# A fused attention and two-layer network: units of 256 tokens, then pairs of 512 with part of g in the place of w_in

## The chip, the cores and the metric

One core of one Trainium2 chip. The metric is device time in microseconds (us) of one execution, from the start of the program to its end; a kernel's time is the median of several runs. The core has TensorE (PE: matmuls; its weight loads are shown as PEld), VectorE (DVE), ScalarE (ACT), GpSimd (POOL) and SyncE (SP), which issues the DMAs here.

## What is computed

Attention with positive random features, then a network of two layers on every token. Cut to what matters:

```python
# q, k, v: [8 batches, 8 heads, 576 tokens, 64]; omega: [128, 64]
def phi(x):                       # x scaled by 64 ** -0.25
    h = x @ omega.T - sum(x * x) / 2
    return exp(h - max(h)) / sqrt(128)
kv = einsum('bhsm,bhsd->bhmd', phi(k), v); z = sum over s of phi(k)
attn = einsum('bhsm,bhmd->bhsd', phi(q), kv) / (phi(q) . z + 1e-6)
x = attn as [4608 tokens, 512]
h = x @ w_in                      # w_in: [512, 2048]
out = (h - tanh(h)) @ w_out       # w_out: [2048, 512]
```

## The kernel before

The 4608 tokens are 18 units of 256 (`TC`), four chunks of 128 features (`NC`) each. w_in and w_out together are 16 tiles `wt[f]` of 128 partitions, each with a coarse part (index 0) and a fine part (index 1) of two float32r numbers whose sum is the weight; a part's first 512 words are a block of w_in (128 columns of h), its last 512 a block of w_out. They are loaded packed (`raw`) and decoded on ACT, DVE and POOL (`decode`, L439 to L451) in the first 160 us.

**The attention** of the later units is made of steps that run beside the network. A `k_unit` (one batch, one chunk; `k_single` after the first two batches) makes the sums kv and z; a `q_unit` (one unit, one chunk) makes 128 features of x for 256 tokens, and `x_split` writes them as a coarse and a fine part into `xh` and `xl` (L406, L407), which hold two units. A k step and a q step are generators: each `yield` ends a stage, and `beat()` lets every running step make one stage. The table `start` says at which beat a step begins; a unit of the network takes 16 beats, and units 0 and 1 are done as one.

**The network** of a unit: `ffn_h` (L468) makes two tiles of h, f = 2s and 2s+1, in 24 matmuls of 256 columns (4 chunks x 3 products x 2 tiles; the weights are `wt`, x is what streams). tanh (ACT, L472), h - tanh(h) (DVE, L473), the coarse part gh (ACT, L474) and the fine part gl (DVE, L475) follow. `ffn_out` (L486 to L488) multiplies g of the step before with w_out: 12 matmuls of 512 columns, into the two output tiles `po0` and `po1` of 128 tokens. Each of the 8 banks of PSUM has its tag. Units 0 and 1, in which no attention needs PSUM any more, are one unit of 512 tokens: one tile of h is 12 matmuls of 512 columns, and there are four output tiles.

**The order of the work** is made by a scheduler, which keeps the program's meaning and sets the order on each engine; each engine then runs in that order, and so does the queue of DMAs on SP.

In a unit, x must be whole before its first tile of h:

```python
while ch > 2 and xdone.get(ch, 0) < NC:
    tick((), True)
g = (ch, s, *ffn_h(ch, s))
```

Of the kernel before, what the change touches and what calls it, by code (L numbers as in the profile page):

```python
# [19 lines left out]
P = 128  # L20
# [1 line left out]
NF = DFF // P  # L22
NS = NF // 2
TC = 256
NCH = NT // TC
E = D + 2
SCALE = float(D) ** -0.25
EPS = 1e-6 * M
# [3 lines left out]
def favor_attention_ffn(ctx: ExitStack, tc: tile.TileContext, qT, kT, va, vt, omT, w, out):  # L32
# [283 lines left out]
    def q_unit(ch, c):  # L316
# [47 lines left out]
        if native:  # L364
            qf = att("qt", [P, 2, TC], F32, f"qt_{n}")
            nc.scalar.copy(qf.rearrange("p h t -> p (h t)"), pt)
            yield
            pn = ps.tile([P, TC], F32, tag=bank("pt"), name=f"pn_{n}")
            for b, s, e in pieces:
                for h in range(2):  # L370
                    nc.tensor.matmul(pn[:, s:e], kvf[b][c][:, h], qf[:, h, s:e], start=h == 0, stop=h == 1)
            if ch == 2:
                if c < 2:
                    x2[c] = sb.tile([P, TC], F32, tag="xs", name=f"x2_{c}", bufs=2)
                elif c == 2:
                    x2[3] = sb.tile([P, DM], F32, tag="o", name="x2")
                    x2[2], x2[3] = x2[3][:, 0:TC], x2[3][:, TC:]
                nc.scalar.copy(x2[c], pn)
# [112 lines left out]

    def ffn_store(ch):
        for t, p in enumerate(pos[ch]):
            if ch == NCH - 1 and t == 1:
                o = sb.tile([P, DM], F32, tag="g", name=f"o_{ch}_{t}")
                nc.vector.tensor_copy(o, p)
            else:
                o = sb.tile([P, DM], F32, tag="o", name=f"o_{ch}_{t}")
                nc.scalar.copy(o, p)
            r = ch * TC + t * P  # L500
            nc.sync.dma_start(out[r : r + P, :], o)
# [50 lines left out]
    while decoded < NF:  # L552
# [26 lines left out]
    mode.update(  # L579
        chain=False, native=False, norm=[nc.vector, nc.vector, nc.vector, nc.scalar], junk=[junk],  # L580
        hi=nc.scalar, pj=["pj0"], pk=["pk"], pt=["pj0"],
        phi=(ak, 3), qh=(ak, 1), ql=(ak, 1), tmp=(ak, 1), kf=(ak, 1), kx=(ak, 1), qf=(ak, 2),
        qx=(ak, 1), vr=(ak, 1), khl=(ak, 2), vhl=(ak, 2), zs=(ak, 1), c1=(ak, 1), kvs=(ak, 1))
# [6 lines left out]
    for b in range(2, B):  # L592
        for c in range(NC):
# [3 lines left out]
    assert min(start) >= t  # L597
# [6 lines left out]
    for s in range(done, NF):  # L604
        step(s, beat)
    for c in range(NC):
        x_split(2, c, x2[c], nc.vector)
    ffn_out(*prev)
    ffn_store(0)
    mode.update(pj=["pj0", "pj1"], pt=["pt"])  # L610
    prev = None
    for ch in range(2, NCH):
        out_tiles(ch)
        for s in range(NS):
            while ch > 2 and xdone.get(ch, 0) < NC:
                tick((), True)
            g = (ch, s, *ffn_h(ch, s))
            beat()
            if prev is not None:
                ffn_out(*prev)  # L620
                if s == 0:
                    ffn_store(ch - 1)
            beat()
            prev = g
    ffn_out(*prev)
    ffn_store(NCH - 1)
    for name in list(pools)[::-1]:
        close_pool(name)

# [34 lines left out]
```

## Time and profile before

| | before |
|---|---|
| median of 3 runs | 1071.04 us (1069.25 to 1071.6) |
| the profiled execution, its own time | 1070.01 us |
| its span in the profile | 1068.2 us |
| PE busy | 1044.0 us (98%), 6760 matmuls |
| PEld busy | 949.3 us (89%) |
| DVE busy | 854.0 us (80%) |
| ACT busy | 713.2 us (67%) |
| POOL busy | 323.5 us (30%) |
| DMA | 55.91 MB, mean 52 GB/s |

Times in the profile are counted from the start of the span. PE's matmuls overlap (the end of one is modelled), so the time that one takes in a row of them is read from start to start, not from its duration. DVE's short operations overlap too: its busy time is less than the sum of their durations. The granted clock (PEclk) is a share of full speed: 1.00 is 2.4 GHz, 0.50 is 1.2 GHz. A group of instructions has the line, engine, operation, out<-in, shape and count, then busy us, mean ns of one, and the idle time before them with what ended it.

### The profile page before, as it was taken

How to read it: one execution, taken by the hardware profiler on the slowest of the kernel's cores; microseconds unless marked ns; L12 is line 12 of the kernel's file. 1: busy time of each engine (PE TensorE's matmuls, PEld its weight loads, DVE VectorE, ACT ScalarE, POOL GpSimd, SP SyncE). 2: the span in 40 equal slices, each digit the busy share in tenths (PEclk: the TensorE clock that was granted, in tenths of full speed). 3: DMA queues.
4: the chain of work that ended last, by engine and by line, in shares of the span. 5: the costliest groups of instructions: out<-in, count | busy, mean ns of one | idle time of the engine just before them, and what ended most of it. 6: DMA issues, size and time to landing. Idle time of an engine off the chain costs nothing. (4 is left out here: it accounts for less than half of the span.)

```text
span 1068.2 us, 20318 instructions
## 1 busy us (share of the span) xinstructions
PE 1044.0 (98%) x6760; PEld 949.3 (89%) x6760; DVE 854.0 (80%) x3030; ACT 713.2 (67%) x1833; POOL 323.5 (30%) x553
## 2 busy tenths in 40 slices
PE   8988999989999999999999999999999999999998
PEld 7767888988999999999999998999999999999997
DVE  6999985898888986788888888898888897666522
ACT  6997655777676765577777766777767775555422
POOL 4634540344333320133333333233333331000000
PEclk8999999998999999999999999999999999999999
DMA  8750401111111110011111111111101110000000
GB/s 266 234 212 12 178 4 48 43 43 38 33 53 33 53 33 31 11 53 33 52 34 52 34 28 53 33 48 29 51 22 52 29 41 11 30 11 26 1 21 20
DMA packets 35529, 55.91 MB, mean 52 GB/s; under 512 B 12256, under 2 KB 21600, under 8 KB 33376
## 3 DMA queue, kind: packets, MB, share of 16 engines
q1 hardware_dynamic: 35344, 54.57, 16.2%
q8 instruction: 54, 0.88, 0.4%
q14 instruction: 51, 0.42, 0.1%
q10 hardware_dynamic: 80, 0.03, 0.0%
HBM read 45.15 MB, written 9.44 MB: 51 GB/s over the span
## 5 line engine op out<-in xcount | busy, mean ns | idle before, releaser
L468 PE MATMUL h<-xh,w 128*128 128x256 f32 (+1 forms) x2176 | 453.3, 292 | 3.8 <-DVE g L473 2.1
L468 PEld LDWEIGHTS h<-xh,w 128*128 128x128 f32 x2176 | 356.7, 191 | 14.1 <-DVE g L473 2.7
L468 PE MATMUL h<-xl,w 128*128 128x256 f32 (+1 forms) x1088 | 317.3, 292 | 0.5 <-DVE xl L407 0.5
L486 PE MATMUL po<-w,gh 128*128 128x512 f32 x544 | 214.2, 394 | 0.0
L468 PEld LDWEIGHTS h<-xl,w 128*128 128x128 f32 x1088 | 207.9, 191 | 6.7 <-DVE xl L407 0.8
L487 PE MATMUL po<-w,gh 128*128 128x512 f32 x544 | 213.7, 393 | 0.0
L488 PE MATMUL po<-w,gl 128*128 128x512 f32 x544 | 209.3, 391 | 0.0
L473 DVE TENSOR_TENSOR g<-h,g 128x512 f32<-128x512 f32 x144 | 98.8, 686 | 66.4 <-ACT g L472 65.3
L472 ACT ACTIVATE g<-h 128x512 f32<-128x512 f32 x144 | 85.1, 591 | 99.2 <-PE h L468 91.9
L474 ACT CAST gh<-g 128x512 fp32r<-128x512 f32 x144 | 89.4, 621 | 84.3 <-DVE g L473 82.7
L475 DVE TENSOR_TENSOR gl<-g,gh 128x512 fp32r<-128x512 f32 x144 | 109.9, 764 | 38.3 <-ACT gh L474 36.5
L488 PEld LDWEIGHTS po<-w,gl 128*128 128x128 f32 x544 | 102.2, 188 | 20.7
L486 PEld LDWEIGHTS po<-w,gh 128*128 128x128 f32 x544 | 102.5, 188 | 16.6
L487 PEld LDWEIGHTS po<-w,gh 128*128 128x128 f32 x544 | 102.5, 188 | 15.2
L347 DVE CUSTOM_DVE_ANT_0 junk<-phi_q,zb 128x128 f32<-128x128 f32 (+1 forms) x320 | 96.5, 303 | 14.7 <-ACT phi_q L150 0.5
L250 POOL TENSOR_TENSOR khl<-phi_ka,khl 128x256 fp32r<-128x256 f32 x48 | 38.0, 795 | 154.2 <-DVE khl L249 129.2
L150 ACT ACTIVATE phi_q<-phi_q,nb_q 128x128 f32<-128x128 f32 x240 | 79.0, 392 | 6.3 <-DVE nb_q L146 6.1
L258 POOL CAST vhl<-v 128x128 fp32r<-128x128 f32 (+1 forms) x144 | 45.7, 319 | 100.9 <-PE pk L266 82.4
L439 POOL TENSOR_SCALAR a<-a 128x1024 f32<-128x1024 f32 x14 | 59.0, 4214 | 54.7 <-ACT a L435 42.1
L387 DVE TENSOR_TENSOR ql<-pt,qh 128x512 fp32r<-128x512 f32 x60 | 41.1, 685 | 26.5 <-ACT qh L386 26.1
L259 DVE TENSOR_TENSOR vhl<-v,vhl 128x128 fp32r<-128x128 f32 (+1 forms) x144 | 45.2, 314 | 16.7 <-POOL vhl L258 13.0
L146 DVE CUSTOM_DVE_ANT_0 phi_q<-pj_q,phi_q 128x128 f32<-128x128 f32 x240 | 55.9, 283 | 1.1 <-ACT phi_q L143 1.0
(151 smaller groups left out, 1952.9 us busy)
## 6 DMA issues: line engine op xcount, KB each, us to landing
raw<-w SPq DMA_DIRECT2D x16, 1024.0 KB, 7.5
kf<-kT SPq DMA_DIRECT2D x32, 288.0 KB, 2.9
qf<-qT SPq DMA_DIRECT2D x72, 128.0 KB, 2.1
out<-o SPq DMA_DIRECT2D x36, 256.0 KB, 2.0
v<-vt SPq DMA_DIRECT2D x24, 288.0 KB, 2.8
v<-va SPq DMA_DIRECT2D x8, 288.0 KB, 5.8
omf<-omT ACTq DMA_DIRECT2D x1, 32.0 KB, 2.1
omf<-omT SPq DMA_DIRECT2D x1, 32.0 KB, 2.4
```

The lines of the kernel that those rows point to most:

```text
L146: nc.vector.tensor_tensor_reduce(ph[:, j], pj[:, i, :M], ph[:, j], scale=-SCALE, scalar=3.0e38, op0=ALU.add, op1=ALU.min, accum_out=nb[:, ...
L150: nc.scalar.activation(ph[:, j], ph[:, j], AF.Exp, bias=nb[:, j : j + 1], scale=-1.0)
L347: nc.vector.tensor_tensor_reduce(bank("junk")[r], ph[r, i], kvs[b, c][1][r, h], scale=1.0, scalar=EPS, op0=ALU.mult, op1=ALU.add, accum_ou ...
L439: engine.tensor_scalar(a.bitcast(F32), a.bitcast(F32), 2.0**-15, 122879.9921875, op0=ALU.max, op1=ALU.min)
L468: nc.tensor.matmul(o, w_, x, start=i == 0, stop=i == len(prods) - 1)
L472: nc.scalar.activation(g, p, AF.Tanh)
L473: nc.vector.tensor_sub(g, p, g)
L474: nc.scalar.copy(gh, g)
L475: nc.vector.tensor_sub(gl, g, gh.bitcast(F32))
L486: nc.tensor.matmul(po[t], h, wt[f][:, 0, DM:], start=first, stop=False)
L487: nc.tensor.matmul(po[t], h, wt[f][:, 1, DM:], start=False, stop=False)
L488: nc.tensor.matmul(po[t], l, wt[f][:, 0, DM:], start=False, stop=last)
```

## The change

Units 0 to 5 (`C0` = 6) stay as they are. The other twelve become six pairs of 512 tokens (`NL`). In a pair, `wide_h` makes one tile of h for all 512 tokens, in 12 matmuls of 512 columns. PSUM has room for two output tiles only, so `wide_out` adds up the output of the pair's first 256 tokens while h is made (6 matmuls of 512 columns per tile of h), and g of the other 256 tokens is kept until h is done: POOL writes its coarse and fine parts over the first half of the block of w_in that has just been used (`wt[f][:, i, 0:TC]`). Two runs of 48 matmuls, one for each of the other two output tiles, follow (`products`). So that the next pair finds w_in again, `w_in_away` stores w_in in DRAM during unit 2, and `w_in_back` loads each block, about six tiles ahead, into the second halves of w_in's places, which hold eight blocks (`NB`).

x of a pair is collected in a new tile `later`; `next_x` splits it when all eight q steps of the pair are there, after the h of the pair before. The table `start` is another one; a pair has 40 beats. Some buffers go or shrink to make room: `xs`, `tmp`, `o` (output tiles of units 0 to 5 use the buffers of gl and gh), `qf` from 2 to 1, `kvw` from 7 to 6.

```diff
-                    xs = sb.tile([P, TC], F32, tag="xs", name=f"xs_{n}", bufs=2)
+        while ch >= C0 and gathered < (ch - C0) // 2:
+            yield
+        xs = later[:, c, ch % 2 * TC : ch % 2 * TC + TC]
...
+    def w_in_away(f):
+        w_dram[f] = tc.dram_tile([P, 2, DM], F32, name=f"w_in{f}")
+        nc.sync.dma_start(w_dram[f], wt[f][:, :, 0:DM].bitcast(F32))
+    def w_in_back(i):
+        f, k = i % NF, 2 * (i % NB)
+        for j in range(2):
+            for a in range(2):
+                nc.sync.dma_start(wt[k + j][:, a, TC:DM].bitcast(F32), w_dram[f][:, a, TC * j : TC * j + TC])
...
+    def wide_h(a, f):
+        p = ps.tile([P, 2, TC], F32, tag=bank("h"), name=f"h_w{a}_{f}")
+        prods = [(w_in(a, f, i, c), x[:, 0:2, c]) for c in range(NC)
+                 for i, x in ((0, xh), (0, xl), (1, xh))]
+        for i, (w_, x) in enumerate(prods):
+            nc.tensor.matmul(p, w_, x, start=i == 0, stop=i == len(prods) - 1)
...
+        nc.scalar.activation(g, p, AF.Tanh)
+        nc.vector.tensor_sub(g, p, g)
+        nc.scalar.copy(e[:, 0], g[:, 0])
+        nc.vector.tensor_sub(e[:, 1], g[:, 0], e[:, 0].bitcast(F32))
+        hi, lo = [wt[f][:, i, 0:TC] for i in range(2)]
+        nc.gpsimd.tensor_copy(hi, g[:, 1])
+        nc.gpsimd.tensor_sub(lo, g[:, 1], hi.bitcast(F32))
...
-            k = 28 + 4 * c if ch == 3 else 42 + 4 * c if ch == 4 else 16 * (ch - 1) - 6 + 4 * c
+            if ch < C0 + 2:
+                k = [(28,32,36,40),(41,45,49,53),(56,60,63,66),(58,68,72,75),(78,81,83,85)][ch - 3][c]
+            else:
+                k = begins(a - 1) + -9 + 10 * (j + c) // 2
             start.setdefault(k, []).append(("q", ch, c))
...
-            k = 31 + 5 * c if b == 2 else 16 * (need[b] - 1) - 25 + 8 * c
+            k = [31,51][b - 2] + [5,5][b - 2] * c if b < 2 + len([31,51]) else begins(a - 1) + -18 + 11 * c
...
+    next_x(0)
+    for a in range(NL):
+        r = (C0 + 2 * a) * TC
+        out_tiles("w")
+        prev = None
+        for f in range(NF):
+            g = wide_h(a, f)
+            beat()
+            if prev is not None:
+                wide_out(*prev)
+            i = NF * a + f + 6
+            if NF <= i < NF * NL:
+                w_in_back(i)
+            beat()
+            prev = g
+        wide_out(*prev)
+        for i in range(2):
+            store(pos["w"][i], r + i * P)
+        for i in range(2):
+            p = ps.tile([P, DM], F32, tag=bank("h"), name=f"last_{a}_{i}")
+            for f in range(NF):
+                products(p, f, *[wt[f][:, j, i * P : (i + 1) * P] for j in range(2)])
+                if f % 4 == 3:
+                    beat()
+            store(p, r + (2 + i) * P, nc.vector if a == NL - 1 and i == 1 else nc.scalar)
+            if i == 0 and a < NL - 1:
+                next_x(a + 1)
```

How the scheduler sets the changed program shows in two places. On PE, at the start of unit 6 before (`po` are output tiles of unit 5, `h` is unit 6's first tile):

```order
L486 MATMUL po_5_4427<-w_1525,gh_6_5045 128x512
L487 MATMUL po_5_4427<-w_1525,gh_6_5045 128x512
L488 MATMUL po_5_4427<-w_1525,gl_6_5046 128x512
L468 MATMUL h_0_5170<-xh,w_219 128x256
L468 MATMUL h_0_5170<-xl,w_219 128x256
L468 MATMUL h_0_5170<-xh,w_219 128x256 x2
L363 MATMUL pt_0_5154<-ident,phi_q_0_5066 128x128
L468 MATMUL h_0_5170<-xl,w_219 128x256
L363 MATMUL pt_0_5154<-ident,phi_q_0_5066 128x128 x3
```

and on PE at the start of the first pair now (`h_w_0` and `h_w_1` are the pair's first two tiles of h, `po` again those of unit 5, `pt` a transpose of a later q step; `w_1569` is the tile f = 14):

```order
L532 MATMUL h_w_0_5642<-xl,w_220 128x512
L532 MATMUL h_w_0_5642<-xh,w_220 128x512
L532 MATMUL h_w_1_5705<-xh,w_337 128x512
L532 MATMUL h_w_1_5705<-xl,w_337 128x512
L532 MATMUL h_w_1_5705<-xh,w_337 128x512
L489 MATMUL po_5_4743<-w_1569,gh_7_5538 128x512
L490 MATMUL po_5_4743<-w_1569,gh_7_5538 128x512
L489 MATMUL po_5_4744<-w_1569,gh_7_5538 128x512
L490 MATMUL po_5_4744<-w_1569,gh_7_5538 128x512
L366 MATMUL pt_2_5267<-ident,phi_q_2_5086 128x128 x4
L532 MATMUL h_w_0_5642<-xh,w_220 128x512
L532 MATMUL h_w_1_5705<-xh,w_337 128x512
```

Before, unit 6's first tile of h followed in the order of its chunks, with nothing but the transposes of one q step among it; now the first pair's first two tiles stand in pieces of a chunk or less, and matmuls of unit 5's last step and of attention have been moved between them.

On SP, the loads of the packed weights f = 8 to 11 before (`qf` is a load for a q step):

```order
L81 DMA raw_987<-w 128x1024
L81 DMA qf_3_1041<-qT 128x256
L81 DMA raw_1084<-w 128x1024
L81 DMA raw_1139<-w 128x1024
L81 DMA raw_1249<-w 128x1024
```

and the same place now (`w_in` is w_in's copy in DRAM, stored from the decoded tiles f = 4 to 7):

```order
L84 DMA raw_1082<-w 128x1024
L512 DMA w_in_2042<-w_743 256x1x512
L512 DMA w_in_2044<-w_905 256x1x512
L512 DMA w_in_2203<-w_983 256x1x512
L512 DMA w_in_2205<-w_1078 256x1x512
L84 DMA raw_1137<-w 128x1024
```

Four stores, each of which needs a decoded tile, stand ahead of the load of f = 10 now.

## Rows read from the trace of the kernel before

**Rows 1.** Page, part 1: busy us (share of the span) and instructions of two engines.

```profile
PE 1044.0 (98%) x6760; PEld 949.3 (89%) x6760; DVE 854.0 (80%) x3030; ACT 713.2 (67%) x1833; POOL 323.5 (30%) x553
```

**Rows 2.** Timeline of PE at 1000 us: start, length, line, operation, count.

```profile
1000.03 0.28 PE L468 MATMUL h<-xl,w 128*128 128x256 f32 x1
...
1001.47 0.28 PE L468 MATMUL h<-xl,w 128*128 128x256 f32 x1
```

**Rows 3.** Timeline of PE in units 0 and 1 (512 tokens), one tile of h.

```profile
128.11 0.39 PE L468 MATMUL h<-xh,w 128*128 128x512 f32 x1
...
130.83 0.39 PE L486 MATMUL po<-w,gh 128*128 128x512 f32 x1
```

**Rows 4.** Timeline of PE at unit 3's start; in brackets the idle time before.

```profile
239.54 0.50 PE L142 MATMUL pj_kb<-om,kx 128*128 128x256 f32 x2 [2.82 <-DVE nb_km L146]
...
241.69 1.09 PE L363 MATMUL pt<-ident,phi_q 128*128 128x128 f32 x4 [1.15 <-DVE xs L400]
```

**Rows 5.** Timeline of DVE: the last chunks of x of units 3 and 6.

```profile
245.78 0.43 DVE L407 TENSOR_TENSOR xl<-xs,xh 128x256 fp32r<-128x256 f32 x1
...
409.18 0.42 DVE L407 TENSOR_TENSOR xl<-xs,xh 128x256 fp32r<-128x256 f32 x1
```

**Rows 6.** Timeline of PE: unit 6's first matmul.

```profile
411.77 0.28 PE L468 MATMUL h<-xh,w 128*128 128x256 f32 x1
```

**Rows 7.** Windows: us, busy of PE, PEld, DVE, ACT, POOL, clock, DMA share, GB/s.

```profile
50.00:100.00 50.00, 41.66 (x223) 33.27 (x222) 49.41 (x162) 42.07 (x114) 18.07 (x8) 1.00 0.32 119
202.60:245.80 43.20, 38.59 (x250) 34.67 (x248) 39.63 (x157) 32.66 (x92) 19.71 (x40) 0.94 0.16 48
245.80:409.20 163.40, 162.94 (x1112) 151.62 (x1113) 142.74 (x559) 114.37 (x308) 56.55 (x109) 0.98 0.14 39
500.00:900.00 400.00, 399.46 (x2742) 370.44 (x2741) 347.47 (x1370) 286.84 (x774) 143.33 (x278) 1.00 0.13 38
900.00:1000.00 100.00, 100.00 (x666) 91.98 (x666) 64.31 (x241) 55.53 (x138) 0.00 (x0) 1.00 0.06 18
245.00:250.00 5.00, 4.47 (x21) 4.18 (x21) 4.92 (x15) 2.71 (x9) 3.52 (x6) 0.50 0.47 121
```

**Rows 8.** Windows of line L400 alone (DVE): one operation for each q step.

```profile
245.80:409.20 163.40, 5.13 (x12) 0.98 0.14 39
900.00:1000.00 100.00, 2.99 (x7) 1.00 0.06 18
```

**Rows 9.** Windows of line L313 alone (DVE): one operation for each k step.

```profile
245.80:409.20 163.40, 2.08 (x6) 0.98 0.14 39
```

**Rows 10.** Windows of line L475 alone (DVE): one for each two tiles of h.

```profile
245.80:409.20 163.40, 17.58 (x23) 0.98 0.14 39
900.00:1000.00 100.00, 11.08 (x16) 1.00 0.06 18
```

**Rows 11.** Page, part 5: the work on h, in groups of the whole run.

```profile
L473 DVE TENSOR_TENSOR g<-h,g 128x512 f32<-128x512 f32 x144 | 98.8, 686 | 66.4 <-ACT g L472 65.3
L472 ACT ACTIVATE g<-h 128x512 f32<-128x512 f32 x144 | 85.1, 591 | 99.2 <-PE h L468 91.9
L474 ACT CAST gh<-g 128x512 fp32r<-128x512 f32 x144 | 89.4, 621 | 84.3 <-DVE g L473 82.7
L475 DVE TENSOR_TENSOR gl<-g,gh 128x512 fp32r<-128x512 f32 x144 | 109.9, 764 | 38.3 <-ACT gh L474 36.5
```

**Rows 12.** Page, part 5: two groups of POOL.

```profile
L250 POOL TENSOR_TENSOR khl<-phi_ka,khl 128x256 fp32r<-128x256 f32 x48 | 38.0, 795 | 154.2 <-DVE khl L249 129.2
...
L258 POOL CAST vhl<-v 128x128 fp32r<-128x128 f32 (+1 forms) x144 | 45.7, 319 | 100.9 <-PE pk L266 82.4
```

**Rows 13.** Timeline of DVE: the last operation of decoding f = 7.

```profile
99.19 1.22 DVE L451 SCALAR_TENSOR_TENSOR w<-m,a 128x1024 fp32r<-128x1024 uint32 x1
```

**Rows 14.** Timeline of ACT: the first operation of decoding f = 10.

```profile
108.18 1.15 ACT L435 ACTIVATE a<-raw 128x1024 f32<-128x1024 f32 x1
```

**Rows 15.** Page, part 6: loads of packed weights, KB each, us to landing.

```profile
raw<-w SPq DMA_DIRECT2D x16, 1024.0 KB, 7.5
```

More of the change, by code (lines that the diff above doesn't have):

```diff
@@ L24 @@
 TC = 256
-NCH = NT // TC
+NQ = NT // TC
+C0 = 6
+NL = (NQ - C0) // 2
+NB = 8
 E = D + 2
@@ L372, in q_unit @@
             if ch == 2:
[L373 to L378, printed above, removed]
+                nc.scalar.copy(later[:, c, 0:TC], pn)
             else:
@@ L456, in favor_attention_ffn @@
     xh, xl = [sb.tile([P, 2, NC, TC], F32R, name=f"x{k}") for k in "hl"]
+    later = sb.tile([P, NC, 2 * TC], F32, name="later")
     def ffn_h(ch, s):
@@ L493, in ffn_store, with store @@
         for t, p in enumerate(pos[ch]):
[L494 to L501, printed above, removed]
+            store(p, ch * TC + t * P)
+    def store(p, r, engine=nc.scalar):
+        o = sb.tile([P, DM], F32, tag=bank("o"), name=f"o_{r}", bufs=1 if mode["o"][-1] == "g" else 2)
+        copy(engine, o, p)
+        nc.sync.dma_start(out[r : r + P, :], o)
@@ L503, in out_tiles, with products, wide_out @@
+    def products(o, f, h, l):
+        nc.tensor.matmul(o, h, wt[f][:, 0, DM:], start=f == 0, stop=False)
+        nc.tensor.matmul(o, h, wt[f][:, 1, DM:], start=False, stop=False)
+        nc.tensor.matmul(o, l, wt[f][:, 0, DM:], start=False, stop=f == NF - 1)
+    def wide_out(a, f, h, l):
+        for t, p in enumerate(pos["w"]):
+            products(p, f, h[:, t * P : (t + 1) * P], l[:, t * P : (t + 1) * P])
     def out_tiles(ch, tags=("po0", "po1")):
@@ L508, in favor_attention_ffn @@
     xdone = {}
-    x2 = {}
+    gathered = 0
     gens = []
@@ L581, in favor_attention_ffn, with begins @@
         hi=nc.scalar, pj=["pj0"], pk=["pk"], pt=["pj0"],
[L582 removed]
+        phi=(ak, 3), qh=(ak, 1), ql=(ak, 1), kf=(ak, 1), kx=(ak, 1), qf=(ak, 1),
         qx=(ak, 1), vr=(ak, 1), khl=(ak, 2), vhl=(ak, 2), zs=(ak, 1), c1=(ak, 1), kvs=(ak, 1))
     start = {}
[L588 removed]
+    def begins(a):
+        return 16 * C0 + 40 * a
+    for ch in range(3, NQ):
+        a, j = (ch - C0) // 2, (ch - C0) % 2 * NC
         for c in range(NC):
[L590 removed]
+            if ch < C0 + 2:
+                k = [(28,32,36,40),(41,45,49,53),(56,60,63,66),(58,68,72,75),(78,81,83,85)][ch - 3][c]
+            else:
+                k = begins(a - 1) + -9 + 10 * (j + c) // 2
             start.setdefault(k, []).append(("q", ch, c))
     for b in range(2, B):
+        a = ((b * S) // TC - C0) // 2
         for c in range(NC):
[L594 removed]
+            k = [31,51][b - 2] + [5,5][b - 2] * c if b < 2 + len([31,51]) else begins(a - 1) + -18 + 11 * c
             start.setdefault(k, []).append(("k", b, c))
     t = 32 - 2 * (NF - done)
[L597 removed]
+    assert min(start) >= t and all(k == int(k) for k in start)
     def beat():
@@ L606, in favor_attention_ffn @@
     for c in range(NC):
-        x_split(2, c, x2[c], nc.vector)
+        x_split(2, c, later[:, c, 0:TC], nc.vector)
     ffn_out(*prev)
@@ L611, in favor_attention_ffn @@
     prev = None
-    for ch in range(2, NCH):
+    for ch in range(2, C0):
         out_tiles(ch)
@@ L622, in favor_attention_ffn @@
                     ffn_store(ch - 1)
+            if ch == 2:
+                for f in range(2 * s, 2 * s + 2):
+                    w_in_away(f)
             beat()
@@ L625, in favor_attention_ffn, with next_x @@
     ffn_out(*prev)
-    ffn_store(NCH - 1)
+    ffn_store(C0 - 1)
+    mode.update(o=["g", "gl"])
+    def next_x(a):
+        nonlocal gathered
+        for ch in (C0 + 2 * a, C0 + 2 * a + 1):
+            while xdone.get(ch, 0) < NC:
+                tick((), True)
+        gathered = a + 1
+        for c in range(NC):
+            x_split(slice(0, 2), c, later[:, c].rearrange("p (j t) -> p j t", j=2), nc.vector)
+    next_x(0)
[25 more added lines that the diff above has]
+                next_x(a + 1)
     for name in list(pools)[::-1]:
```

32 lines of the change are left out of this document (21 added, 11 removed).

## The prediction, made blind

> **What bounds the kernel now.** I read the busy line of the page first: PE 98%, DVE 80% [rows 1]. The windows say where: from 500 to 900 us PE is busy for 399.5 of 400 us at full clock, and DVE for 347.5 [rows 7]. So there PE's work sets the time, and a change must take work from PE. It must also keep PE fed, for DVE is not far behind. The timeline of PE shows the one place after the opening where it isn't: at unit 3's start PE idles 2.82 and then 1.15 us for DVE [rows 4], and then runs at a granted clock of 0.50, 1.2 GHz, from 245 to 250 us [rows 7]. The reader is to see that this stall ends when DVE writes unit 3's last chunk of x at 245.8 us [rows 5]. DVE was busy for 39.6 of the 43.2 us before that, 0.917, and could go no faster with that mix of work [rows 7].
>
> **What the change takes from PE.** In the timeline, 12 matmuls of h with 256 columns take 1001.47 - 1000.03 = 1.44 us, 0.120 each [rows 2]. In units 0 and 1, which already have 512 columns, 12 take 130.83 - 128.11 = 2.72 us, 0.2267 each [rows 3]. Twelve units had 12 x 192 = 2304 of the first kind; six pairs have 6 x 192 = 1152 of the second. 2304 x 0.120 = 276.5 us becomes 1152 x 0.2267 = 261.2 us: **-15.3 us**. All of it lies on PE, which bounds. The second layer keeps its 192 matmuls of 512 columns per 512 tokens (16 x 6 while h is made and 2 x 48 after it, against 2 x 8 x 12 before), and attention keeps all of its.
>
> Against this stands a page of the Trainium skill. "TensorE: Matmul & The Clock Gate", section "Wait — 56ns, not 53.3ns?", gives a matmul in a row one clock per column and about 2.5 ns more. By that a pair would save 1152 x 2.5 ns = 2.9 us in all, an estimate from the page. The rows disagree with it: two matmuls of 256 columns are 0.240 us and one of 512 is 0.227, so here the part that doesn't grow with the columns is 13 ns, and I take the rows.
>
> **What it costs: the way into the first pair.** A unit needed its own x; the first pair needs x of units 6 and 7 before its first tile of h is whole. The new table and the scheduler's list put 16 q steps and about 8 k steps between unit 3's last chunk of x and the pair's last one. Before, 12 q and 6 k steps [rows 8, 9] and 23 double tiles of h [rows 10] lay between unit 3's last chunk (245.8 us) and unit 6's (409.2 us) [rows 5]. So DVE has 4 q steps, 2 k steps and one double tile more to do there.
>
> A double tile is 0.686 + 0.764 = 1.45 us of DVE [rows 11]. From 900 to 1000 us no k step runs: (64.3 - 16 x 1.45) / 7 = 5.9 us for a q step [rows 7, 8, 10]. From 245.8 to 409.2 us: (142.7 - 12 x 5.9 - 23 x 1.45) / 6 = 6.4 us for a k step. More: 4 x 5.9 + 2 x 6.4 + 1.5 = 38 us. DVE needs 142.7 + 38 = 181 us for the stretch.
>
> How fast it does them is the unknown. It has been busy for 0.988 of a stretch, decoding from 50 to 100 us, and for 0.917 when PE waited for it at unit 3 [rows 7]. That gives 183 or 197 us. I take 0.94, nearer to the second, since the work and the waits are of that kind: 193 us.
>
> PE took 411.8 - 245.8 = 166 us from there to unit 6's first matmul [rows 5, 6]. Four q steps (12 small matmuls, at most 0.12 each) and two k steps (23) add 4 x 1.4 + 2 x 2.8 = 11 us. Between the pair's first matmul and the last x that it needs, the scheduler has put 9 wide matmuls of f = 0, 9 of f = 1 and unit 5's last 12 output matmuls, 30 x 0.227 = 7 us. So PE has 184 us of work and waits 193 - 184 = 9 us; bounds 0 and 13. A stall at half clock behind it, as at unit 3: in 245 to 250 us 4.5 us of work ran at 0.50 [rows 7], 2.3 us lost. I add 2.5, bounds 0 and 7.5 (three such stalls, as the list is in pieces at units 4 and 5 too). **+11.5 us**. The PE work pulled forward is not lost, the waiting is.
>
> **What I cost at nothing, and its cover.**
> - Unit 3's start: DVE's list ahead of its last x is the same but for about 3 us less. 0, bounds -5 and 0.
> - The opening: on SP the store of f = 7 must wait for its decoding, over at 100.4 us [rows 13], and the load of f = 10 is now behind it. ACT wants that load at 108.2 us [rows 14]; a load takes 7.5 us to land [rows 15]: 100.4 + 0.5 + 7.5 = 108.4. Cover is PE's backlog of network work at that time. 0, bounds 0 and 5.
> - g in a pair: tanh 0.59, difference 0.69, then half-size parts, 0.31 and 0.38: 2.0 us [rows 11]. Cover: 6 + 12 matmuls, 4.1 us. Without it PE would wait at each of 96 tiles.
> - POOL gets two operations of 256 columns per tile. The nearest are 0.795 us for a difference and twice 0.319 for a copy [rows 12]: 16 x 1.43 = 23 us per pair, on top of 0.36 x 104 = 37 us [rows 7], out of 104. Nobody waits for them but the buffers of g, two tiles later, and the tail of the pair.
> - DVE in a pair: 0.87 x 107 = 93 us before [rows 7]; halving gl saves 16 x 0.38 = 6. If each of POOL's 32 operations held up DVE by 0.25 us it would give 8 back: 95 of 104.
> - From one pair to the next, x can't be split before the last h. Cover: 6 + 96 matmuls, 23 us, of which DVE's list fills up to 22. 0, bounds 0 and 5 over five pairs.
> - 64 loads of 128 KB per pair on SP are 8 MB in 104 us, 80 GB/s; 50 to 100 us had 119 GB/s at a DMA share of 0.32 [rows 7]. They go out six tiles, some 35 us, ahead.
> - Output tiles of units 2 to 5 in the buffers of gh and gl, `qf` with one buffer: 0, bounds 0 and 2.
>
> **The sum.** -15.3 + 11.5 = -3.8 against the profiled execution's 1070.0 us: **1066 us**. That execution is 1.0 below the median of 1071.0, so as a change of the median it is half a per cent. About 0.2%, 2.1 us, is what a measurement here tells from no change.
>
> **The rivals.**
> 1. *DVE keeps pace.* It held 0.988 before [rows 7]; then it needs 183 us, PE's 184 bound, and at most a short wait is left: -15.3 + 0 to 3, so 1055 to 1058. For it: POOL and DMA don't hinder it more than there. Against: PE and DVE wait for each other in turn here, and at unit 3 that gave 0.917.
> 2. *Slower: DVE bounds from unit 3 to the first pair.* At 0.917 PE waits 13 us, and with the half clock behind stalls at units 4, 5 and the pair another 7.5: -15.3 + 20.5 = +5, 1075. It decides once the pair's last x comes later than 245.8 + 184 + 17.4 - 2.5 = 445 us, where 17.4 is 15.3 and the 2.1 that can be told. For it: the list already shows pieces at three starts, where before only unit 3 had them, and there PE stalled. Against: DVE did 0.87 to 0.91 with PE never waiting.
> 3. *POOL or x late in every pair.* 3 us in each of six pairs, +18: 1084. Against: POOL has 40% left.
> 4. *Two of 256 columns cost no more than one of 512* when nothing else changes, so the change doesn't do what it is for: +11.5, 1081. Against: the durations of [rows 2, 3]. The Trainium skill's rule above leans this way.
>
> **How the numbers follow.** Forecast (1062 to 1070): 0.45, of which 0.33 is faster by over 2.1 us and 0.12 within it. Rival 1: 0.20. Rival 2: 0.25, of which 0.03 is within 2.1 us. Rivals 3 and 4: 0.06 and 0.04. Faster 0.53, same 0.15, slower 0.32. The range 1056 to 1077 takes in the forecast and nearly all of rivals 1 and 2.
>
> **What would show it.** Right: in a pair 12 matmuls of h in 2.7 us; PE without gaps inside pairs; a stall of 5 to 13 us, summed over units 4 and 5 and the first pair's start, that ends on DVE's x; the pair's last x near 436 us. Wrong: no idle PE there (rival 1), x after 445 us and several stretches at 0.50 (rival 2), gaps at each pair whose releaser is POOL or xl (rival 3), 2.9 us for 12 matmuls (rival 4), or a stall before 200 us for decoded weights, which I cost at nothing.

## The result, and the profile after the change

The changed kernel takes 1075.36 us (median of 5 runs, 1074.22 to 1076.49) against 1071.04: a ratio of 1.0046, 95% interval 1.0031 to 1.0061. It is slower, by somewhat under half a per cent; forecast was 1066 us, faster. The profiled execution has a span of 1073.6 us against 1068.2, so 5.4 us are to be found. Line numbers are now 3 higher than before up to the end of the q step.

The first part of the page, as in [rows 1]:

```profile
PE 1041.5 (97%) x5608; PEld 889.1 (83%) x5608; DVE 854.3 (80%) x3006; ACT 695.0 (65%) x1809; POOL 440.9 (41%) x745
```

PE has 1152 matmuls fewer and yet is busy for only 2.5 us less, and its idle time grew from 1068.2 - 1044.0 = 24.2 to 1073.6 - 1041.5 = 32.1 us. POOL does 117 us more.

**The matmuls themselves** are what the forecast took them for. The timeline of PE in the last pair, where no attention is left:

```profile
982.58 0.39 PE L532 MATMUL h_w<-xh,w 128*128 128x512 f32 x1
...
990.29 0.39 PE L532 MATMUL h_w<-xl,w 128*128 128x512 f32 x1
```

34 matmuls start in these 7.71 us, 0.2268 each, as in [rows 3].

**The way into the first pair.** The timeline of DVE shows unit 3's last chunk of x and, behind those of units 4 and 5, the pair's four:

```profile
238.89 0.42 DVE L408 TENSOR_TENSOR xl<-later,xh 128x256 fp32r<-128x256 f32 x1
...
417.48 0.69 DVE L408 TENSOR_TENSOR xl<-later,xh 128x512 fp32r<-128x512 f32 x1
422.19 0.69 DVE L408 TENSOR_TENSOR xl<-later,xh 128x512 fp32r<-128x512 f32 x1
430.57 0.68 DVE L408 TENSOR_TENSOR xl<-later,xh 128x512 fp32r<-128x512 f32 x1
438.16 0.69 DVE L408 TENSOR_TENSOR xl<-later,xh 128x512 fp32r<-128x512 f32 x1
```

Unit 3's last chunk now comes at 238.9 us (the tanh of unit 3's first tiles follows at 242.7), 6.9 us earlier than before the change [rows 5]. The pair's last one comes at 438.2 us; 436 was forecast. PE, meanwhile, runs out of work on unit 5 at 424 us and waits (timeline of PE; in brackets the idle time before, and who ended it):

```profile
427.34 0.36 PE L145 MATMUL pj_km<-om,kx 128*128 128x256 f32 x1 [0.83 <-DVE nb_ka L149]
428.35 0.48 PE L145 MATMUL pj_q<-om,qx 128*128 128x256 f32 x2 [0.66 <-DVE nb_ka L149]
429.39 0.50 PE L269 MATMUL pk<-khl,vhl 128*128 128x256 f32 x2 [0.56 <-POOL khl L253]
...
436.50 0.63 PE L366 MATMUL pt<-ident,phi_q 128*128 128x128 f32 x4 [1.10 <-DVE later L399]
...
438.91 0.50 PE L532 MATMUL h_w<-xl,w 128*128 128x512 f32 x1 [0.89 <-DVE xl L408]
...
443.27 0.50 PE L532 MATMUL h_w<-xh,w 128*128 128x512 f32 x1 [1.94 <-DVE g_w L536]
```

Windows of the same places and of two stretches inside the pairs (us, busy of PE, PEld, DVE, ACT, POOL, clock, DMA share, GB/s):

```profile
238.89:438.16 199.27, 190.88 (x1265) 171.77 (x1263) 182.69 (x739) 151.25 (x409) 76.56 (x148) 0.99 0.15 43
440.00:445.00 5.00, 3.06 (x15) 2.37 (x14) 4.88 (x17) 4.71 (x13) 1.72 (x3) 0.91 0.62 185
445.00:450.00 5.00, 5.00 (x18) 3.96 (x17) 4.72 (x10) 1.55 (x4) 3.90 (x7) 0.75 0.19 61
450.00:565.00 115.00, 115.00 (x602) 97.76 (x601) 103.50 (x397) 80.86 (x223) 61.20 (x117) 1.00 0.28 84
565.00:680.00 115.00, 114.02 (x595) 95.84 (x594) 102.61 (x399) 79.24 (x218) 61.35 (x113) 1.00 0.38 115
```

The way from unit 3's last chunk to the pair's last one took 199.3 us, where the forecast had 193. DVE was busy for 182.7 us of it, where the forecast had 181: a share of 0.917, not 0.94, and just that of unit 3's stall in [rows 7]. Behind the stall some of PE's work runs at half clock (a mean of 0.75 from 445 to 450 us). Inside the pairs DVE is busy for 0.90 of the time, where it was 0.87 [rows 7].

**Inside the pairs** PE waits too. Before the change, no wait for g is listed there. After it, the four largest waits of PE and of its weight loads (PEld) from 450 us on are for g (us in total, times, longest):

```profile
PEld po_w L547 <- DVE ge_w L538: 2.8, 4, 1.1
PEld h_w L532 <- DVE g_w L536: 2.1, 4, 1.1
PE po_w L547 <- DVE ge_w L538: 1.2, 2, 0.7
PE h_w L532 <- DVE g_w L536: 0.7, 1, 0.7
```

Waits this short are often hidden in the modelled ends of the matmuls. So I add up **lost time** instead: from each matmul's start to the next one's, less its columns at 2.4 GHz and 13.5 ns. (By [rows 2, 3] 256 columns take 0.120 and 512 take 0.2267 us; 13.3 and 13.4 ns of these are not columns.) Idle time, half clock and short waits all count as lost. The times without lost time are 975.2 us before and 959.7 after; the 15.5 between them are 1152 x 13.5 ns by this definition, no measurement of their own. Lost time by stretch of the span, in us:

| kernel | to 182 | 182 to 440 | 440 to 552 | 552 to end | sum |
|---|---|---|---|---|---|
| before | 56.7 | 16.7 | 1.7 | 12.7 | 87.8 |
| after | 58.5 | 24.3 | 6.6 | 19.3 | 108.7 |

Of the 20.9 us that were given back, 12.5 lie between 182 and 552 us, the way into the first pair and its start, and 6.6 in the pairs behind that. The 12.5 are a difference of two things. From 182 us to unit 3's last chunk of x (245.8 us before, 238.9 after) 8.7 us were lost before and 1.0 after, 7.6 less, as unit 3's stall is gone; from that chunk to 552 us it was 9.7 before and 29.9 after, 20.1 more. The 1.8 before 182 us I don't count against the change: the kernels below that have the same opening lost 55.9 to 58.2 there, so single profiles differ by that much.

### The profile page after: what moved, and what is told of

Read it like the earlier page. It is cut to its first block, busy times and chain, and to the rows that moved or that the text cites. A ratio compares the mean times of both kernels' runs of the same rounds, so it can differ in the third digit from the quotient of the medians.

```text
span 1073.6 us, 19114 instructions
## 1 busy us (share of the span) xinstructions
PE 1041.5 (97%) x5608; PEld 889.1 (83%) x5608; DVE 854.3 (80%) x3006; ACT 695.0 (65%) x1809; POOL 440.9 (41%) x745
## 4 chain that ended last, share of the span: by engine, by line
PE 67%; DVE 22%; issue 5%; ACT 4%; POOL 1%; DMA 0%; DVEq 0%; POOLq 0%; ACTq 0%
PE h_w L532 19%; PE h L471 7%; PE last L545 4%; PE last L547 4%; PE last L546 4%; DVE junk L350 3%; PE po_w L547 3%; PE po_w L546 3%; PE po_w L545 3%; PE po L489 2%; PE po L490 2%; PE po L491 2%; PE pk L269 2%; PE pt L366 2%; DVE phi_q L359 2%
## 5 line engine op out<-in xcount | busy, mean ns | idle before, releaser
L532 PE MATMUL h_w<-xh,w 128*128 128x512 f32 x768 | 253.9, 394 | 2.7 <-DVE g_w L536 2.6
L532 PEld LDWEIGHTS h_w<-xh,w 128*128 128x128 f32 x768 | 144.1, 189 | 31.1 <-DVE g_w L536 4.2
L532 PE MATMUL h_w<-xl,w 128*128 128x512 f32 x384 | 151.3, 394 | 0.9 <-DVE xl L408 0.9
L471 PE MATMUL h<-xh,w 128*128 128x256 f32 (+1 forms) x640 | 147.2, 307 | 3.8 <-DVE g L476 2.2
L471 PEld LDWEIGHTS h<-xh,w 128*128 128x128 f32 x640 | 107.5, 190 | 11.8 <-DVE g L476 3.1
L471 PE MATMUL h<-xl,w 128*128 128x256 f32 (+1 forms) x320 | 97.5, 305 | 2.1 <-DVE xl L408 2.1
L532 PEld LDWEIGHTS h_w<-xl,w 128*128 128x128 f32 x384 | 72.8, 190 | 14.4 <-DVE xl L408 1.3
L541 POOL TENSOR_TENSOR w<-g_w,w 128x256 fp32r<-128x256 f32 x96 | 80.0, 833 | 4.6
L545 PE MATMUL po_w<-w,ge_w 128*128 128x512 f32 x192 | 75.9, 395 | 0.0
L545 PE MATMUL last<-w 128*128 128x512 f32 x192 | 75.4, 393 | 0.0
L546 PE MATMUL po_w<-w,ge_w 128*128 128x512 f32 x192 | 75.3, 392 | 0.0
L547 PE MATMUL last<-w 128*128 128x512 f32 x192 | 75.2, 392 | 0.0
L546 PE MATMUL last<-w 128*128 128x512 f32 x192 | 75.1, 391 | 0.0
L547 PE MATMUL po_w<-w,ge_w 128*128 128x512 f32 x192 | 72.2, 395 | 1.3 <-DVE ge_w L538 1.2
```

Of the source, the lines that this page charges most:

```text
L471: nc.tensor.matmul(o, w_, x, start=i == 0, stop=i == len(prods) - 1)
L532: nc.tensor.matmul(p, w_, x, start=i == 0, stop=i == len(prods) - 1)
L541: nc.gpsimd.tensor_sub(lo, g[:, 1], hi.bitcast(F32))
L545: nc.tensor.matmul(o, h, wt[f][:, 0, DM:], start=f == 0, stop=False)
L546: nc.tensor.matmul(o, h, wt[f][:, 1, DM:], start=False, stop=False)
L547: nc.tensor.matmul(o, l, wt[f][:, 0, DM:], start=False, stop=f == NF - 1)
```

## The experiments

All edits are to the changed kernel. The kernel before ran again beside each of them, with medians from 1070.4 to 1071.3, so a difference of two rows can be off by some 0.8 us. The table has their lost time, and for some the **path of g**: from the end of a tile's last matmul of h to the end of DVE's ge_w (L538, the fine part of g's first half), a mean over the tiles from 455 to 850 us.

| run | us | 182 to 440 | 440 to 552 | 552 to end | path of g |
|---|---|---|---|---|---|
| after | 1075.36 | 24.3 | 6.6 | 19.3 | 5.8 |
| e2_halves | 1089.68 | 27.4 | 4.7 | 19.3 | |
| e8_nox0 | 1079.61 | 17.4 | 14.8 | 24.3 | |
| e1_norm | 1079.62 | 26.3 | 9.3 | 20.6 | 6.3 |
| e3_nopool | 1068.51 | 24.6 | 6.2 | 13.5 | 4.6 |
| e10_dvelo | 1070.47 | 26.6 | 4.0 | 15.6 | 5.2 |
| e14_lodve | 1075.06 | 26.0 | 6.5 | 18.2 | 6.0 |
| e20_memset | 1071.65 | 26.7 | 4.1 | 16.0 | 5.4 |
| e21_other | 1079.18 | 27.2 | 5.7 | 22.7 | 6.1 |
| e5_noreload | 1072.77 | 26.1 | 5.6 | 17.1 | 5.7 |
| e9_c8 | 1072.11 | 17.4 | 7.3 | 21.1 | |
| e11_c8dvelo | 1066.05 | 17.8 | 7.3 | 14.5 | |
| e12_c8n | 1067.95 | 10.1 | 14.0 | 16.1 | |

### What the width is worth: e2_halves

```diff
-        prods = [(w_in(a, f, i, c), x[:, 0:2, c]) for c in range(NC)
+        for r in range(2):
+            prods = [(w_in(a, f, i, c), x[:, r, c]) for c in range(NC)
...
+                nc.tensor.matmul(p[:, r], w_, x, start=i == 0, stop=i == len(prods) - 1)
```

> The changed kernel, but each tile of h in a pair as 2 x 12 matmuls of 256 columns in place of 12 of 512. Nothing else differs, so it prices the width alone. Account: the wide ones had 226.4 ns each in the pairs and two narrow ones take 2 x 121.3, so 1152 x 16.2 ns = 18.7 us more, less what of the 7 us of waits inside the pairs it covers: 1086 to 1094 us. Rival (the width saves nothing, or 2.9 us, and the loss lies elsewhere): 1075 to 1079 us.

1089.68 us, 14.3 above the changed kernel, at equal lost time. So the width gives 14.3 us, or 12.4 ns for each matmul saved, and the loss lies elsewhere. The rival that it saves nothing falls.

### The way into the first pair: e8_nox0, e1_norm

```diff
-            while xdone.get(ch, 0) < NC:
+            while a and xdone.get(ch, 0) < NC:
...
-        for c in range(NC):
+        for c in range(NC if a else 0):
             x_split(slice(0, 2), c, ...
```

> The changed kernel, but the first pair's h is made from the x of units 4 and 5 that lies in xh and xl already; the split of units 6 and 7 into them is left out, all their q and k steps stay. So only the wait of the first pair for its x goes. Account: PE lost 11.0 us between 367 and 440 us and 4.1 between 440 and 450, against some 3 in the same place before the change; with the wait gone about 12 of these 15 us go, the stall at unit 5's start (2.3 us at 365 us) stays: 1062 to 1066 us. Rival (DVE's backlog isn't gone by this and PE waits for it in the first pair's tiles): 1070 to 1075 us.

1079.61 us: both theories missed, the rival by less. The first pair started without a wait, but the steps that were still to be done went on to the second pair's start. Two windows of this run, columns as above:

```profile
520.00:540.00 20.00, 17.55 (x91) 14.16 (x90) 14.63 (x54) 13.46 (x37) 9.16 (x17) 0.98 0.22 71
540.00:565.00 25.00, 19.10 (x75) 14.82 (x76) 24.27 (x103) 18.76 (x52) 10.41 (x23) 0.67 0.24 73
```

PE is busy for 19.1 of 25 us there, at a mean clock of 0.67, while DVE is busy for 24.3. The price of the way in is therefore work that must be done by then, not one wait: leave out the wait, and it comes 100 us later and dearer.

```diff
-norm=[nc.vector, nc.vector, nc.vector, nc.scalar]
+norm=[nc.vector, nc.scalar]
```

> The changed kernel, with two instead of three of every four products of phi and dn on DVE (the other two on ACT). Account so far: the changed kernel is 5 us slower since -15.5 us of columns are outweighed by +12 on the way into the first pair, where DVE can't get through 16 q and some 8 k steps in PE's time, +7 of small waits for DVE inside the pairs, and +1.8 before 182 us. By that, DVE is rid of 16 x 0.34 = 5.5 us before the first pair's last x (438.2 us), which then comes near 433, and of 0.34 us per q step inside the pairs: 1066 to 1071 us. Rival (DVE isn't what the way in waits for, or ACT becomes late in its place): 1074 to 1077, with the last x at 437 us or later.

1079.62 us, slower than either theory had it. The first pair's last x came at 439 us, no earlier. Between 300 and 440 us DVE's busy time fell from 127.6 to 123.8 us, and PE lost 26.3 instead of 24.3 between 182 and 440. So DVE's busy time alone isn't what the way in waits for. The steps pass through DVE, ACT and PE in turn, and I take it that ACT put in again what DVE was spared (its busy time from 300 to 440 us rose from 106.1 to 108.7); that wasn't tried by itself. ACT also makes tanh and the cast of g, and the path of g got longer, 6.3 us.

### POOL's two operations on g: e3_nopool, e10_dvelo, e14_lodve, e13_pool2

```diff
-        nc.gpsimd.tensor_copy(hi, g[:, 1])
-        nc.gpsimd.tensor_sub(lo, g[:, 1], hi.bitcast(F32))
```

> The changed kernel without POOL's two operations on g in the pairs; so the upper and lower part of the second half of g are left out, and the last two output tiles of each pair are made from other numbers. Account: DVE's ge_w took 544 ns beside POOL and should take some 400; with that and the other operations of DVE shorter, the 7 us of waits inside the pairs fall to 2 or less: 1067 to 1071 us. Nothing changes before the first pair (last x at 438 us). Rival (DVE's own list is long enough to be late): 1074 to 1076 us.

1068.51 us, as the account had it, 6.9 less; ratio to before 0.9976, interval 0.9966 to 0.9985. Only the pairs changed: 13.5 us lost behind 552, about as before the change. So POOL's operations, which the forecast priced at nothing, cost 6.9 us. Groups by line, from 450 us on, in the changed kernel (count, busy us, mean ns, idle before):

```profile
L538 DVE TENSOR_TENSOR ge_w<-g_w,ge_w 128x256 fp32r<-128x256 f32 x94 | 51.0, 544 | 15.6 <-ACT ge_w L537 14.2 <-PE pj_q L145 0.5
```

The same group in this run:

```profile
L538 DVE TENSOR_TENSOR ge_w<-g_w,ge_w 128x256 fp32r<-128x256 f32 x94 | 44.3, 472 | 15.4 <-ACT ge_w L537 14.8
```

The same operation of DVE takes 544 ns with POOL's and 472 without. Summed over all of DVE's operations after 450 us the difference is 24.7 us.

Sorted by the matmul that came late, the lost time behind 552 us is:

| kernel | h | output | attention | sum |
|---|---|---|---|---|
| before | -0.4 | 2.7 | 10.4 | 12.7 |
| after | 2.5 | 4.6 | 12.1 | 19.3 |
| e3_nopool | 2.0 | 2.0 | 9.5 | 13.5 |

(It falls a little below 0 where the 13.5 ns are a little too much.) Of the 6.6 us that the change added, 4.8 stand at the network's matmuls, h and output. Of the 5.8 that POOL's operations cost here, 2.6 stand at the output's, which wait for g, and as much at attention's: the path of g is not all of their price.

```diff
-        nc.gpsimd.tensor_copy(hi, g[:, 1])
-        nc.gpsimd.tensor_sub(lo, g[:, 1], hi.bitcast(F32))
+        nc.scalar.copy(hi, g[:, 1])
+        nc.vector.tensor_sub(lo, g[:, 1], hi.bitcast(F32))
```

> The changed kernel with POOL's cast of g's second half on ACT and POOL's difference on DVE. Two theories of the 6.9 us that the run without POOL's operations saved. A, POOL's operations lengthen DVE's where both run at once (ge_w 544 ns for 256 columns): then DVE does one operation of some 0.4 us more per tile, 38 us in all, but 0.15 us less on ge_w and less on others, so its busy share in the pairs stays near 0.9 and the time within 3 us of the changed kernel's: 1072 to 1078. B, DVE's list is too long in the pairs, whatever makes it so: DVE gets longer by some 25 us net and PE waits more: 1080 to 1092 us.

1070.47 us, 4.9 less, below both ranges and level with the kernel before (ratio 0.9998, interval 0.9990 to 1.0007). DVE got 96 operations more and still the path of g became shorter; DVE's other operations took 31 us less. The same view of this run:

```profile
L541 DVE TENSOR_TENSOR w<-g_w,w 128x256 fp32r<-128x256 f32 x94 | 49.9, 530 | 0.1
L538 DVE TENSOR_TENSOR ge_w<-g_w,ge_w 128x256 fp32r<-128x256 f32 x94 | 44.7, 476 | 13.3 <-ACT ge_w L537 12.0
```

Theory B, DVE's length, falls. With the difference alone moved to DVE:

```diff
-        nc.gpsimd.tensor_sub(lo, g[:, 1], hi.bitcast(F32))
+        nc.vector.tensor_sub(lo, g[:, 1], hi.bitcast(F32))
```

> The changed kernel with POOL's difference (833 ns) on DVE and POOL's cast (427 ns) left where it is. The run that moved both saved 4.9 us though DVE's busy time rose. If the two-input difference on POOL is what hinders DVE, this one saves as much: 1069 to 1072 us. If both hinder in proportion to their time, two thirds of it: 1071 to 1074. If the gain came from ACT's doing the cast, nothing: 1074 to 1077.

1075.06 us: nothing gained, although DVE's other operations took 20 us less, and nothing lost, although DVE has 25 us more to do in all. The path of g is 6.0 us, much as without the edit. This is the third theory's range: the gain of e10_dvelo came only with the cast gone from POOL too. Shorter operations of DVE didn't bring it here, and why the cast, the smaller of the two, decides is not shown.

With both operations done twice on POOL:

```diff
         nc.gpsimd.tensor_copy(hi, g[:, 1])
+        nc.gpsimd.tensor_copy(hi, g[:, 1])
         nc.gpsimd.tensor_sub(lo, g[:, 1], hi.bitcast(F32))
+        nc.gpsimd.tensor_sub(lo, g[:, 1], hi.bitcast(F32))
```

> The changed kernel with POOL's two operations on g done twice each (same numbers written again). If POOL's work costs time by what it does to DVE's operations at the same moment, twice the work costs about as much again as leaving it out saved (6.9 us): 1079 to 1085 us. If the saving came from another order of the lists, or from a buffer that POOL frees late once, doubling adds little: 1074 to 1078 us.

1107.19 us, far over. Here something new waits, ACT's tanh for the buffer of g that POOL reads last (waits from 450 to 1070 us: in total, times, longest; L543 is the second difference):

```profile
ACT g_w L535 <- POOL w L543: 19.6, 12, 2.6
```

The run shows how steep the price of POOL gets, and no more: it doesn't tell one way from another.

### By what way POOL costs: e20_memset, e21_other, and four that didn't tell

```diff
+        nc.gpsimd.tensor_copy(hi[:, 0:64], g[:, 1, 0:64])
+        for _ in range(4):
+            nc.gpsimd.memset(hi.bitcast(F32), 0.0)
-        nc.gpsimd.tensor_copy(hi, g[:, 1])
-        nc.gpsimd.tensor_sub(lo, g[:, 1], hi.bitcast(F32))
```

> The changed kernel, but POOL casts only 64 columns of g's second half, so that it still waits for g, and then, in place of the rest, fills the same tile four times with zeros (0.28 us each, 1.1 us, against 1.26 us for cast and difference); so the last two output tiles of each pair are made from other numbers. POOL's load and its place in the list are about as in the changed kernel, but it reads and writes little beside DVE. If the 6.9 us come from DVE's operations being lengthened by POOL's (L): 1067 to 1070 us, as without them. If they come from POOL's being late or waiting for g (its queue): 1073 to 1077.

```diff
+        nc.gpsimd.tensor_copy(hi[:, 0:64], g[:, 1, 0:64])
+        nc.gpsimd.tensor_copy(hi, om2.bitcast(F32))
+        nc.gpsimd.tensor_sub(lo, om2.bitcast(F32), hi.bitcast(F32))
-        nc.gpsimd.tensor_copy(hi, g[:, 1])
-        nc.gpsimd.tensor_sub(lo, g[:, 1], hi.bitcast(F32))
```

> The changed kernel with the same 64 columns of g cast first, and then POOL's cast and difference at full size on a constant tile in place of g; so the last two output tiles of each pair are made from other numbers. Load, wait for g and reading beside DVE are as in the changed kernel or a little more (0.15 us per tile); only g's buffer comes free some 1.2 us earlier. If that buffer is what costs: 1067 to 1071 us. By L or by POOL's queue: 1074 to 1080.

1071.65 us, between its two ranges, and 1079.18. POOL was busy even a little longer with the memsets (a cast of 271 ns and four of 315 per tile, against 427 and 833), waited for g as before, and yet 3.7 of the 6.9 us were gained; DVE's operations took 18 us less. With POOL reading another tile nothing was gained, rather 3.8 lost. The two runs are the cleanest pair: POOL's work per tile is 1.53 and 1.51 us, both wait for g in the same place and both free g's buffer early, and yet they lie 7.5 us apart. So about half of POOL's price goes when it stops reading beside DVE, and g's buffer is no part of it. The other 3 us lie between POOL's load and the order of the lists, and stay open.

The Trainium skill, "SBUF — State Buffer", section "Who interferes with whom", says that a VectorE instruction with two inputs in SBUF contends with a GpSimd one that reads SBUF, and not with one that only writes. The rows agree: ge_w, whose two inputs lie in SBUF, has 544 ns beside POOL's two operations on g, 584 in e21_other, 498 beside the memsets (with the cast of 64 columns, which still reads) and 472 without; g's first difference, which has one input in PSUM, has 686 or 687 ns in all of them.

Four more were to tell a late POOL from longer operations of DVE. The base, and on it a fourth phi buffer, the edit of e10_dvelo, and that edit with two operations of POOL's that nobody waits for:

```diff
-kvw=(sb, 6), zb=(sb, 6)
+kvw=(sb, 5), zb=(sb, 5)
```

> The changed kernel with five in place of six buffers each for kvw and zb: the base for the next three runs, which need the 2 KB. No theory expects much of it: 1074 to 1079 us.

```diff
-phi=(ak, 3)
+phi=(ak, 4)
```

> The base with a fourth buffer of phi. Open is by what way POOL's two operations on g cost their 6.9 us. Theory H: POOL comes to its old operations later, so that it reads phi later, and ACT, which waits for that buffer (5.6 us of waits for POOL's khl after 450 us, none before the change), holds g's tanh and casts behind it. By H a fourth buffer takes those waits away and saves 3 to 7 us against the base. Theory L: POOL's operations only lengthen DVE's beside them (25 to 31 us of DVE's time after 450 us). By L: within 1.5 us of the base.

> The base with POOL's two operations on ACT and DVE, as in the run that saved 4.9 us. Base for the next: 4 to 6 us less than the first of these four.

```diff
+    sa = sb.tile([P, TC], F32R, name="sa")
...
+        nc.gpsimd.tensor_copy(sa, om2.bitcast(F32))
+        nc.gpsimd.tensor_sub(sa, om2.bitcast(F32), sa.bitcast(F32))
```

> The run before, with two operations of POOL's added per tile, of the old sizes, on a tile that nothing else reads or writes. They wait for nobody and nobody waits for them, but they load POOL and stand beside DVE's operations as the old ones did. By L, or if POOL's own queue gets late, it costs 4 us or more against the run before. If only the order of g through POOL costs (g's buffer, the wait for g at the head of POOL's queue), it costs under 1.5 us.

1084.54, 1084.96, 1084.62 and 1116.63 us. The base was a bad one: a buffer less of kvw and zb costs 9 us, with 28.0 us lost behind 552, and on it neither the fourth phi buffer nor the moved operations change anything. In the last run the scheduler put all of the scratch operations, which depend on nothing, ahead of 350 us, half of them into the opening, where the lost time rose to 76.7 us. None of the three comparisons says anything of H or L. The change itself takes kvw from seven buffers to six; what that costs wasn't tried. Inside the pairs little is left for it: e3_nopool, with six too, lost only 0.8 us more behind 552 than the kernel before.

### The copy of w_in in DRAM: e5_noreload

```diff
-                for f in range(2 * s, 2 * s + 2):
-                    w_in_away(f)
...
-                w_in_back(i)
```

> The changed kernel without the stores of w_in to DRAM and without loading it again, so that from the second pair on h is made from other numbers in w_in's place. Account: transfers are hidden: 1073 to 1076 us, with the lost time before 182 us at 56 to 58. Rival (the traffic of 100 GB/s slows DVE, ACT or PE, or the stores in the opening cost the 1.8 us there): 1066 to 1072 us.

1072.77 us, 2.6 less: between the two ranges, so transfers aren't hidden whole. The stores cost nothing in the opening (58.2 us lost there); the loads, which bring the stretch from 565 to 790 us from 41 to 116 GB/s, cost some 2 us behind 552. By what way isn't shown: DVE's operations are only 2.5 us shorter in sum without them.

### Later pairs: e4_c8, e9_c8, e11_c8dvelo, e12_c8n

With `C0 = 8` the first pair has two more units ahead of it. The first table of starts:

```diff
-C0 = 6
+C0 = 8
-k = [(28,32,36,40),(41,45,49,53),(56,60,63,66),(58,68,72,75),(78,81,83,85)][ch - 3][c]
+k = [(28,32,36,40),(42,46,50,54),(57,61,64,67),(66,76,80,84),(86,89,92,94),(97,100,103,106),(110,113,115,117)][ch - 3][c]
-k = [31,51][b - 2] + [5,5][b - 2] * c if b < 2 + len([31,51]) else begins(a - 1) + -18 + 11 * c
+k = [31,59,81][b - 2] + [5,5,8][b - 2] * c if b < 5 else begins(a - 1) + -18 + 11 * c
```

> The changed kernel with pairs from the ninth unit on (C0 = 8: five pairs in place of six) and starts of q and k steps spread to match. Account: the work that the first pair pulls forward is the same, but DVE has two units (some 106 us) more to get through it and was busy for only 0.86 of them before; so the stall of 24 us of lost time between unit 3 and the first pair falls to 8 or less, and one pair fewer gives back 2.6 us: 1060 to 1068 us. Rival (the way into a pair has a price of its own, wherever it starts): 1076 to 1079 us.

1082.52 us. It squeezed unit 6's steps so far forward that some of unit 4's tiles were made from unit 6's x (DVE wrote its first chunk at 349 us, and unit 4's h was made until 356); and PE lost 31.4 us from 182 to 552, no less than after the change. In e9_c8 the rows for units 5 to 9 are (57,61,65,69), (72,76,80,84), (88,91,94,97), (86,99,102,105), (108,111,114,116), and the k steps start at 31, 55 and 79 (5, 5 and 8 beats apart):

> As the run with C0 = 8, with another table: no step is put earlier than before the change up to unit 6, and units 8 and 9 take the room between beats 84 and 117. If the way in is dear because steps of two more units are squeezed between unit 3 and unit 5, PE's lost time between 182 us and the first pair (some 545 us) is 14 us or less, and the time 1064 to 1070. If two units' x at one start are dear wherever the start lies, PE loses 10 us or more at the pair's start and the time is 1076 to 1083 us.

1072.11 us, between the two. From 182 to 552 us PE lost 24.7 us, against 30.9 with six pairs and 18.4 before the change. Spreading takes away half of what the way in adds.

> Both edits that helped alone: pairs from the ninth unit on with the table that was spread (-3.3 us alone), and POOL's two operations on ACT and DVE (-4.9 alone). If the losses on the way in and inside the pairs are separate, the sum: 1066 to 1069 us, less than the kernel before. If DVE is one pool of time for both, the gains don't add: 1070 to 1073.

**1066.05 us**, ratio 0.9953, interval 0.9940 to 0.9965: 5 us less than the kernel before, with nothing left out. The two gains add (3.3 and 4.9 alone, 9.3 together). The third table, with units 5 and 6 as before the change, (58,62,66,70) and (74,78,82,86), and units 7 to 9 at (88,92,95,98), (100,103,105,108), (111,113,115,117), k steps from 31, 55 and 84 (5, 7 and 7 apart):

> As the run with both edits, but with starts as they were before the change up to unit 6 and the steps of units 8 and 9 all behind unit 7's. If PE's waits at units 5 and 6 come from steps put ahead of theirs, these go (they were 12 us of lost time between 315 and 440 us) and the stall gathers at the first pair: 1064 to 1069 us. If DVE's and ACT's lists are full over the whole way in, the stall at the pair is as large as what is saved: 1069 to 1073.

1067.95 us. The time lies where the first theory put it, but the trace bears out the second: the waits at units 5 and 6 went (10.1 us lost up to 440) and came back from 440 to 552 us (14.0, of which 8.5 from 530 on, around the pair's start), 24.1 in sum, against 25.1 with the other table.

## Why the prediction was wrong

The sum was -15.3 + 11.5 + 0 = -3.8 us; the two profiles show -15.5 (matmuls) + 20.1 (the way into the first pair) - 7.6 (unit 3's stall) + 6.6 (inside the pairs) + 1.8 (the opening) = +5.4.

- **The matmuls, -15.3:** right, 14.3 in e2_halves. The rule of the Trainium skill ("TensorE: Matmul & The Clock Gate", section "Wait — 56ns, not 53.3ns?") would have given 2.9; the run goes with the rows.
- **What failed: "What I cost at nothing", g in a pair.** It set 2.0 us of operations against a cover of 4.1, and "PE without gaps inside pairs" was to be a sign of being right. The operations do take some 2.3 us. But they stand in the lists of ACT and DVE behind attention's: in the changed kernel the path of g took 5.8 us in the mean and up to 9.3. The cover is longer too, with attention's matmuls between: the first output matmul of a tile, which needs only the coarse part of g, follows 6.5 us after the last of h, and the first that needs ge_w's fine part (L547) about 1 us later. To that one 1.6 us were left in the mean, and under 0.6 in 11 of 57 tiles; without POOL's operations it was 2.8, and none. POOL's operations, whose only price was to be 8 us of DVE's slack, are 6.9 us of the end in e3_nopool, about half of it at the network's matmuls.
- **What failed too: how fast DVE goes on the way into the first pair, +11.5.** DVE's work was right (182.7 us, forecast 181), its share was not: 0.917, where the forecast took 0.94 between two measured values. PE lost 20.1 us more there than before the change; the places are 315 to 365 us, up to unit 5's start (8.0 lost), and 424 to 450, around the pair's (12.4). What holds DVE at 0.917 is not shown: in e1_norm less work on DVE didn't help.
- **Unit 3's start, 0 within -5 to 0:** -7.6, outside its bounds. Its last chunk came 6.9 us earlier, and the stall ahead of it went. That the two together, 12.5, look like the forecast's 11.5 is luck, and so is the pair's last x at 438 for 436: the way began 6.9 us earlier and took 6.3 longer.
- **DVE in a pair, 95 of 104:** near (0.90), and not enough as a measure. e10_dvelo loads DVE more and is faster. The lost time behind 552 us goes rather with the path of g in the table, from 4.6 and 13.5 us to 6.1 and 22.7, e14_lodve and e1_norm a little out of line; that is a common course of two numbers, not a test.
- **w_in's reload, 0:** 2.6 us in e5_noreload. It can't be added to POOL's 6.9, as the pairs behind 552 us lost only 6.6 more than before in all.
- **The rivals.** Rival 2 had the way in right: DVE at 0.917 and 20.5 us, where 0.917 and 20.1 were measured. Its sign, a last x after 445 us, counted from unit 3's old chunk and so didn't come. Its time, 1075, came by luck: the 7.6 us given back at unit 3 and the 8.4 lost in the opening and the pairs, neither of which it has, cancel. Rival 3 named POOL, as late in every pair; the largest waits there end on DVE, and the price is 6.9 instead of 18 us.

## What to carry to other kernels

Slack is to be read on the path and not on the engine: add the queueing in each in-order list to the operations' own times before a chain is called covered, for here 2 us of work took 5.8. An operation moved to a POOL that has time left is not free where DVE's work beside it reads two operands from SBUF: here two per tile cost 6.9 us. Where two measured rates of an engine differ, take that of the same mix of work and not a value between. And a batch that needs its inputs earlier pulls their work forward; leave it a longer run-up, since a skipped wait only comes later.

## What the runs showed of the hardware

A matmul of this type has 12 to 13 ns that don't grow with its columns: 0.2268 us for 512 and 0.120 for 256, and 14.3 us more in e2_halves for 1152 matmuls more. POOL's memsets leave DVE's difference of two operands in SBUF (ge_w) nearly as short as leaving out POOL's work on g (498 and 472 ns), its casts and differences don't (544 and 584). And half the operation isn't half the time: with 256 columns DVE's difference takes 472 ns or more, where [rows 11] have 764 for 512 and the forecast took 0.38 us.
